# A gated delta-rule recurrence and a softplus feed-forward on one core: 64-row products for second halves, output transposes on TensorE, one queue for keys, and a new instruction order

## The chip, the cores and the metric

The kernel runs on one NeuronCore of a Trainium2 chip. The metric is the device time of one launch in microseconds (us). Engines are named as in the profile: PE is TensorE (its weight loads are listed apart as PEld), DVE is VectorE, ACT is ScalarE, POOL is GpSimd, SP is SyncE, which here only issues transfers. A letter q behind a name (SPq, POOLq) is the engine's queue of instructions that issue transfers or wait.

## The reference

Four batches of eight heads carry a 48 x 48 state through 768 steps; the gated readouts of all heads form 3072 rows of 384, which go through a feed-forward layer with softplus.

```python
k_n = k / (np.linalg.norm(k, axis=-1, keepdims=True) + 1e-06)
state = zeros((B, H, D, D))                       # B, H, S, D = 4, 8, 768, 48
for t in range(S):
    y[:, :, t] = g[:, :, t] * einsum('bhd,bhde->bhe', q[:, :, t], state)
    v_old = einsum('bhde,bhd->bhe', state, k_n[:, :, t])
    state = state + beta[t] * einsum('bhd,bhe->bhde', k_n[:, :, t], v[:, :, t] - v_old)
x = y.transpose(0, 2, 1, 3).reshape(B * S, H * D)  # 3072 x 384
h = x @ w_in                                       # w_in 384 x 2048
out = (maximum(h, 0) + log1p(exp(-abs(h)))) @ w_out   # w_out 2048 x 384
```

All inputs and the output are float32.

## The kernel before

Time is cut into 12 chunks of 64 steps. Within a chunk, the dependence of each step on earlier steps of the same chunk is a triangular system of 64 unknowns; its matrix comes from the gram products of the keys (tile kkm), and it is solved by an inverse that is built for two chunks at a time: of the two 32-step halves of each chunk directly (tile td), and of the coupling of the second half to the first by a product (tile z). Then a chain runs through the chunks: readout of the state by the keys (w), inverse times w (u), product with z, new u, new state (s), and the gated output (yg). Finally the gated output is transposed (xt), and the dense layer runs on it: `g1` products into h, softplus on ACT into ga, `g2` products into o, copy (osb), store.

Every piece of work is an item. Items carry the cost that was reckoned with when the order was made; emission follows a fixed list of words, a letter for the engine and the item's number. The cost has no effect on the instructions.

```python
def follow(self, table):
    for word in table.split():
        it = self.items[int(word[1:])]
        en = self.ENGINES[word[0]]        # P: PE, D: DVE, A: ACT, G: POOL, S: SP
        it.eng = en
        for b in it.bufs:                 # buffers are taken from rings in this order
            if b.ap is None:
                b.ap = b.ring.free.pop(0)
        it.fn(en) if it.alt else it.fn()
        # ... cut: buffers given back to their rings, counts of items
```

Each engine executes its own items strictly in the order of the list. Loads bring one chunk of q, k, v or g in two transfers of 192 KB each; weights follow on the queue of POOL, each behind a named load.

```python
BY_ACT = (("k", 0), ("k", 2))
FIRST = (("k", 1), ("k", 0), ("k", 2), ("k", 3), ("q", 0), ("v", 0), ("g", 0), ("v", 1), ("q", 1), ("g", 1))
W_IN = (("q", 0), ("q", 0), ("v", 0), ("v", 0))
W_OUT = (("v", 1), ("v", 1), ("q", 1), ("q", 1))
Y_DMA = 4
# ...
r_kn = ring("kn", 4, [P, 2, H, 64], F16, init=pad0)
r_k = ring("kf", 3, [P, 2, H, D], F32)
r_q = ring("qf", 2, [P, 2, H, D], F32)
r_v = ring("vf", 3, [P, 2, H, D], F32)
r_g = ring("gf", 3, [P, 2, H, D], F32)
r_z = ring("z", 3, [P, U, HC], F16)
r_xt = ring("xt", 2, [P, 4, 3, P], F16)
p_d = ring("d", 5, [P, 512], F32, psum)
p_h = ring("h", 2, [P, 512], F32, psum)
p_o = ring("o", 1, [P, 512], F32, psum)
# ... in load():
(nc.scalar if (name, c) in BY_ACT else nc.sync).dma_start(
    out=b.ap[64 * b2 : 64 * b2 + 64].rearrange("t p h d -> t (p h) d"),
    in_=x[2 * b2 : 2 * b2 + 2, :, t0 : t0 + C].rearrange("p h t d -> t (p h) d"),
)
```

The inverse of a pair of chunks runs in steps of two operations, on DVE for the first pair, on POOL for the others. The pair of chunks 8 and 9 takes the wide form of 31 steps:

```python
def step(j):                               # wide form, POOL
    n, w = 31 - j, j + 1
    t = tmp.ap[:, : n * w].rearrange("p (i c) -> p i c", c=w)
    nc.gpsimd.tensor_tensor(t, nn.ap[:, j + 1 :, j : j + 1].broadcast_to([P, n, w]),
                            tt.ap[:, j : j + 1, :w].broadcast_to([P, n, w]), ALU.mult)
    nc.gpsimd.tensor_tensor(tt.ap[:, j + 1 :, :w], tt.ap[:, j + 1 :, :w], t, ALU.add)

for j in range(31):
    prev = add("POOL", "step", 0.52 + 3.2e-3 * (31 - j) * (j + 1), lambda j=j: step(j), deps=[prev], ...)
```

The z-products (`zmm`). The identity puts td of the second half into the second-half rows of z; the kernel before does not read those rows:

```python
for r in range(2):
    f = QUAD[2 * r + 1]                    # rows 32..63 and 96..127
    nc.tensor.matmul(o[f], ident[f, f], td.ap[f, 16 * cl : 16 * cl + 16])   # 512 columns
for u in range(16):
    for r in range(2):
        nc.tensor.matmul(o[QUAD[2 * r], u],
                         kk_low(cs[0], kk, QUAD[2 * r + 1], 16 * cl + u),
                         td.ap[QUAD[2 * r + 1], 16 * cl + u, :])
```

The chain of one chunk. QUAD are the four groups of 32 partitions, HALF the two of 64; m is one of two calls each:

```python
def umm(m):                                # 32 products
    for pi in range(H):
        u = 16 * cl + 2 * pi + m
        for qd in range(4):
            nc.tensor.matmul(hd(up[m].ap)[QUAD[qd], pi], td.ap[QUAD[qd], u, :],
                             w1[m].ap[QUAD[qd], pi], start=(pi == 0), stop=False, ...)
# u1 = copy(up) on ACT or DVE
def zu(m):                                 # 16 products, added to up
    for pi in range(H):
        for r in range(2):
            nc.tensor.matmul(hd(up[m].ap)[QUAD[2 * r + 1], pi],
                             z.ap[QUAD[2 * r], 16 * cl + 2 * pi + m, :],
                             u1[m].ap[QUAD[2 * r], pi], start=False, stop=(pi == H - 1), ...)
# u2 = copy(up); smm: new state from u2; ymm: output; y: yg = output * g
```

The transpose of the gated output, and the dense layer:

```python
if c < Y_DMA or last:                      # chunks 0 to 3 and 11
    for p in range(2):
        def ytr(ytp=ytp, p=p):             # three 128x128 transposes on PE
            for j in range(3):
                nc.tensor.transpose(o[:, cs_], y[:, cs_], ident)
        # then xt: one copy of 128x384 on DVE or ACT
else:                                      # chunks 4 to 10
    nc.sync.dma_start(out=xt.ap[:, 2 * cl : 2 * cl + 2].rearrange("f p j t -> f (p j) t"),
                      in_=yg.ap.rearrange("t p h d -> t (p h d)"), transpose=True)
# g1: 3 products of 128x512 (pairs of chunks) or 6 of 128x256 (single chunks), 96 groups in all
# soft: Softplus on ACT, 128x512
# g2: 4 products of 128x384, 96 groups in all; o: copy on DVE or ACT; store: two transfers
```

Chunks 0, 1, 10 and 11 go through the dense layer singly, the others in pairs.

## Time and profile before

| | before |
|---|---|
| time, median of 3 | 277.19 us (276.89 to 277.89) |
| span of the profiled execution | 275.1 us, 13296 instructions |
| PE busy | 226.1 us (82%), 6030 products |
| DVE, ACT, POOL busy | 165.7 (60%), 134.8 (49%), 141.1 us (51%) |
| dense products: `g1` (h), `g2` (o) | 77.2 and 71.3 us busy, 384 each |
| softplus (ga) | 56.7 us busy, 96 operations |
| moved by DMA | 29.07 MB, 106 GB/s on average |

Busy time is from the first start to the last end of overlapping instructions of an engine; PE's products are pipelined, so that a group of them takes less than its count times the mean of one. Lines such as L236 and L238 are those of a helper that copies on ACT or on another engine, so they are told apart by their tiles (out<-in). "Idle before" is time in which the engine stood still just ahead of a group, with what ended it.

### The profile page before, as it was taken

Reading aid. Unit: us, or ns where it says so; the run is one execution under the profiler, and the core shown is the slowest. Engines: PE = TensorE matmul, PEld = TensorE weight load, DVE = VectorE, ACT = ScalarE, POOL = GpSimd, SP = SyncE. Lnnn points to the kernel's source line nnn. Section 1 sums busy time; section 2 is a strip of 40 time slices with the busy share of each in tenths; the row PEclk is TensorE's granted clock in tenths of the full one; section 3 lists DMA queues with packets and bytes.
Section 4 is the critical chain, followed back from the end, with each engine's and each line's share of the span. In section 5 each row is a group of like instructions: output and inputs, shape, how many; then the busy total and the mean of one; then the engine's idle time right before and its main releaser. Section 6 shows DMA issues by size and latency. Waiting matters only on the chain.

```text
span 275.1 us, 13296 instructions
## 1 busy us (share of the span) xinstructions
PE 226.1 (82%) x6030; PEld 150.5 (55%) x6030; DVE 165.7 (60%) x318; ACT 134.8 (49%) x230; POOL 141.1 (51%) x247
## 2 busy tenths in 40 slices
PE   0540357969898879999999999997599999999986
PEld 0430246757666555555665666553356655668754
DVE  6498589588996626896779956691757123412000
ACT  2241635433764357967447567154536356235620
POOL 8660023888917885287844788888887000000000
PEclk9999999995999979999999999999599999999999
DMA  8999999999998948455993146653312303400312
GB/s 109 144 174 193 173 164 156 181 175 150 142 160 140 135 75 169 84 104 97 151 150 61 33 90 122 116 115 59 64 27 62 76 17 63 84 14 20 71 46 61
DMA packets 113304, 29.07 MB, mean 106 GB/s; under 512 B 106464, under 2 KB 113248, under 8 KB 113248
## 3 DMA queue, kind: packets, MB, share of 16 engines
q1 hardware_dynamic: 105120, 24.19, 53.6%
q0 software_dynamic: 3968, 3.25, 7.6%
q10 hardware_dynamic: 4160, 0.79, 2.4%
q8 instruction: 47, 0.77, 1.2%
q14 instruction: 9, 0.07, 0.1%
HBM read 25.26 MB, written 4.72 MB: 109 GB/s over the span
## 4 chain that ended last, share of the span: by engine, by line
PE 39%; POOL 23%; DVE 11%; DMA 8%; issue 7%; SPq 6%; ACT 3%; DVEq 0%; POOLq 0%; ACTq 0%
PE o L1224 13%; PE h L1194 13%; SPq L268 6%; POOL t L685 6%; POOL tmp L679 6%; DMA qf<-in_q_dram 6%; POOL tt L753 4%; POOL tmp L746 4%; DVE kkm L599 3%; DMA gf<-in_g_dram 2%; PE d L1006 2%; PE d L1043 1%; DVE ln L713 1%; PE d L951 1%; PE d L882 1%
## 5 line engine op out<-in xcount | busy, mean ns | idle before, releaser
L1194 PE MATMUL h<-xt,w_in 128*128 128x512 f16 (+1 forms) x384 | 77.2, 338 | 0.9 <-ACT xt L236 0.6
L1208 ACT ACTIVATE ga<-h 128x512 f16<-128x512 f32 x96 | 56.7, 598 | 40.6 <-PE h L1194 39.3
L1224 PE MATMUL o<-w_out,ga 128*128 128x384 f16 x384 | 71.3, 329 | 1.3 <-DVE osb L238 0.7
L1224 PEld LDWEIGHTS <-ga 128*128 128x128 f16 x384 | 35.8, 98 | 24.4 <-issue 1.9
L1194 PEld LDWEIGHTS <-w_in 128*128 128x128 f16 x384 | 35.6, 101 | 22.6 <-issue 3.3
L433 PE MATMUL d<-ident,kn 128*128 128x128 f16 x96 | 9.4, 258 | 19.6 <-ACT kn L236 10.0
L753 POOL TENSOR_TENSOR tt<-tt,tmp 128x30 f32<-128x30 f32 (+7 forms) x60 | 23.1, 385 | 4.7
L746 POOL TENSOR_TENSOR tmp<-nn,tt 128x30 f32<-128x30 f32 (+7 forms) x60 | 22.0, 367 | 4.5
L236 ACT ACTIVATE u<-d 128x384 f16<-128x384 f32 x28 | 13.3, 492 | 21.8 <-PE d L1043 10.9
L236 ACT ACTIVATE kqx<-d 128x512 f16<-128x512 f16 x27 | 15.0, 593 | 16.2 <-PE d L433 13.4
L599 DVE TENSOR_TENSOR kkm<-d,both 128x512 f16<-128x512 f32 x32 | 20.5, 676 | 2.1 <-PE d L589 2.1
L236 ACT ACTIVATE osb<-o 128x384 f32<-128x384 f32 x19 | 9.3, 489 | 25.2 <-PE o L1224 23.1
L995 DVE TENSOR_TENSOR w<-vf,d 128x384 f16<-128x384 f32 x22 | 11.4, 548 | 15.3 <-ACT ga L1208 11.0
L330 POOL TENSOR_TENSOR ksq<-kf 128x768 f32<-128x768 f32 x6 | 9.1, 1522 | 22.3 <-DMA gf<-in_g_dram 18.5
L433 PEld LDWEIGHTS <-kn 128*128 128x128 f16 x96 | 7.5, 116 | 22.6 <-ACT kn L236 11.8
L238 DVE CAST u<-d 128x384 f16<-128x384 f32 x20 | 10.8, 553 | 14.1 <-PE d L1006 9.4
L363 POOL TENSOR_TENSOR nv<-nv,half_c 128x32 f32<-128x32 f32 x3 | 16.3, 5445 | 5.4 <-DVE nv L340 5.4
L685 POOL TENSOR_TENSOR t<-t,tmp 128x31 f32<-128x31 f32 (+15 forms) x31 | 17.1, 551 | 2.4
L679 POOL TENSOR_TENSOR tmp<-n,t 128x31 f32<-128x31 f32 (+15 forms) x31 | 16.7, 539 | 2.4
L1128 DVE TENSOR_TENSOR yg<-d,gf 128x384 f16<-128x384 f32 x24 | 12.4, 550 | 6.3 <-PE d L1106 6.3
L238 DVE COPY osb<-o 128x384 f32<-128x384 f32 x5 | 2.8, 553 | 20.8 <-PE o L1224 20.8
L1093 DVE TENSOR_TENSOR s<-d,s 128x384 f16<-128x384 f32 x20 | 10.4, 551 | 7.8 <-PE d L1076 7.8
(112 smaller groups left out, 376.8 us busy)
## 6 DMA issues: line engine op xcount, KB each, us to landing
qf<-in_q_dram SPq DMA_DIRECT2D x24, 192.0 KB, 5.6
vf<-in_v_dram SPq DMA_DIRECT2D x24, 192.0 KB, 5.6
gf<-in_g_dram SPq DMA_DIRECT2D x24, 192.0 KB, 4.7
out_dram<-osb SPq DMA_DIRECT2D x48, 96.0 KB, 3.1
kf<-in_k_dram SPq DMA_DIRECT2D x20, 192.0 KB, 5.6
w_in<-in_moe_w_in_dram POOLq DMA_DIRECT2D x4, 384.0 KB, 10.8
w_out<-in_moe_w_out_dram POOLq DMA_DIRECT2D x4, 384.0 KB, 6.5
kf<-in_k_dram ACTq DMA_DIRECT2D x4, 192.0 KB, 6.0
```

Source lines behind the costliest of these rows:

```text
L236: nc.scalar.activation(o, x, AF.Copy, scale=float(sign))
L268: (nc.scalar if (name, c) in BY_ACT else nc.sync).dma_start(out=b.ap[64 * b2 : 64 * b2 + 64].rearrange("t p h d -> t (p h) d"), in_=x[2 * ...
L363: nc.gpsimd.tensor_tensor(x, x, half_c[:, sl], ALU.pow)
L433: nc.tensor.transpose(f16ps(tp.ap)[:, P * i : P * i + P], n.ap.rearrange("t p h d -> t (p h d)")[:, P * i : P * i + P], ident,)
L599: nc.vector.tensor_tensor(kkm.ap[:, u0 : u0 + 7 : 2], gb[m].ap.rearrange("p (n t) -> p n t", t=2 * C), both[:, None, :].broadcast_to([P, N ...
L679: nc.gpsimd.tensor_tensor(t, nn.ap[:, j + 1 :, j : j + 1].broadcast_to([P, n, w]), tt.ap[:, j : j + 1, :w].broadcast_to([P, n, w]), ALU.mult,)
L685: nc.gpsimd.tensor_tensor(tt.ap[:, j + 1 :, :w], tt.ap[:, j + 1 :, :w], t, ALU.add)
L746: eng.tensor_tensor(t, nn.ap[:, :, j + 1 :, j : j + 1].broadcast_to([P, 2, n, w]), tt.ap[:, :, j : j + 1, 16 : 16 + w].broadcast_to([P, 2, ...
L753: eng.tensor_tensor(rows, rows, t, ALU.add)
L1194: nc.tensor.matmul(hp.ap[:, n * b : n * b + n], w_in[:, j, f * P : (f + 1) * P], xt.ap[:, t0 // P : (t0 + n) // P, j], start=(j == 0), sto ...
L1208: lambda hp=hp, o=gb: nc.scalar.activation(o.ap, hp.ap, AF.Softplus),
L1224: nc.tensor.matmul(op.ap[:, :DM], b.ap[:, col + c0 : col + c0 + 128], w_out[:, f, :], start=(f == 0), stop=(f == NF - 1),)
```

## The change

Four parts:

1. The inverse of the second half of a chunk is no longer applied by a separate 32-row product. `umm` forms first halves only and copies the second half of w through with an identity; `zu` then multiplies 64 rows of z, whose second-half rows hold td, with 64 rows of u1, and writes the second half of u afresh instead of adding to it.
2. The gated outputs of chunks 4 to 10 are transposed on PE and copied by DVE or ACT, as those of the other chunks were; the DMA transposes go.
3. The keys of chunks 0 and 2 are loaded by the queue of SP like all others, not by that of ACT.
4. Two cost constants of the inverse's steps are raised, and the list of words is a new one: on each engine the items stand in another order, some items go to another engine (copies, casts, squares, scalings of v), and the rings' buffers are dealt out accordingly.

```diff
-    BY_ACT = (("k", 0), ("k", 2))
+    BY_ACT = ()
...
-    Y_DMA = 4
+    Y_DMA = 12
...
-                "POOL", "step", 0.52 + 3.2e-3 * (31 - j) * (j + 1), lambda j=j: step(j),
+                "POOL", "step", 0.67 + 3.2e-3 * (31 - j) * (j + 1), lambda j=j: step(j),
...
-                en, "step", (0.42 if on_dve else 2 * fix) + 4 * per * (15 - j) * (j + 1), lambda j=j: step(j),
+                en, "step", (0.42 if on_dve else 0.6) + 4 * per * (15 - j) * (j + 1), lambda j=j: step(j),
...
         def umm(m):
+            for r in range(2):
+                f = QUAD[2 * r + 1]
+                nc.tensor.matmul(hd(up[m].ap)[f], ident[f, f], w1[m].ap[f])
             for pi in range(H):
                 u = 16 * cl + 2 * pi + m
-                for qd in range(4):
-                    nc.tensor.matmul(
-                        hd(up[m].ap)[QUAD[qd], pi],
-                        td.ap[QUAD[qd], u, :],
-                        w1[m].ap[QUAD[qd], pi],
-                        start=(pi == 0),
-                        stop=False,
-                        skip_group_check=True,
-                    )
+                for r in range(2):
+                    f = QUAD[2 * r]
+                    nc.tensor.matmul(hd(up[m].ap)[f, pi], td.ap[f, u, :], w1[m].ap[f, pi])
...
                 for r in range(2):
                     nc.tensor.matmul(
                         hd(up[m].ap)[QUAD[2 * r + 1], pi],
-                        z.ap[QUAD[2 * r], 16 * cl + 2 * pi + m, :],
-                        u1[m].ap[QUAD[2 * r], pi],
-                        start=False,
-                        stop=(pi == H - 1),
-                        skip_group_check=True,
+                        z.ap[HALF[r], 16 * cl + 2 * pi + m, :],
+                        u1[m].ap[HALF[r], pi],
                     )
...
 _TABLE = """
-S1 S0 A3 D111 P112 A2 D104 P105 G134 D135 A114 D107 A113 G132 S8 D133 A106 P115 P108 S6 D110 S9
-...
+S1 S0 A111 P112 A114 D113 P115 S3 S2 D104 A132 P105 A116 D133 S5 S4 D197 P198 A117 D107 A106 P108
+...
 """
```

The list has 1137 words before and 1158 after. Of what it changes, these places bear on the prediction (a name with the number of its chunk, or of the first of its pair; cast, red, w, s, y, kev and so on are the copies and operations named above):

```text
SP, before:   k1 k1 q0 k3 q0 k3 q1 v0 v0 g1 q1 g1 k4 q2 g0 g0 q4 q4 q2 k4 v1 v1 ...   (ACT: k0 k0, later k2 k2)
SP, after:    k1 k1 k0 k0 k2 k2 q0 q0 q1 q1 v0 v0 k3 q4 k3 g0 q4 k4 k4 v1 g0 q2 ...
DVE, before:  ... 15 steps of the first inverse, tn, t, cast q1, xs, w0, kkm, w0, red, z0, ln2 ...
DVE, after:   kev1 cast-k0 red cast-k2 kev0 ... 15 steps, tn, t, xs, w0 w0, td, kkm, mask, mask, red, z0 ...
POOL, before: square, square, 2 weight loads, square, 3 weight loads, square, cast k4, ...
POOL, after:  square, 3 weight loads, cast q4, weight load, cast k4, square, clear, weight load, ...
PE, groups of the dense layer + other groups before:    gram 9     z-products of 8    end
   before:                                              56 + 119   108 + 152          192 + 197
   after:                                               56 + 121   108 + 161          192 + 211
```

## The prediction

> **What bounds the kernel now.** I read the slices of the span first, to see which engine is busy when; then the windows of 10 us, for the idle time of TensorE; then the chain of work that ended last and the waits, for what ends that idle time; then the timeline at those places.

> ```profile
> PE   0540357969898879999999999997599999999986
> POOL 8660023888917885287844788888887000000000
> PEclk9999999995999979999999999999599999999999
> DMA  8999999999998948455993146653312303400312
> ```

> A slice is 6.88 us. TensorE is nearly empty for six slices (41 us), part filled to slice 15 (104 us), then full to the end but for a notch at slices 28 and 29. GpSimd is busy until just after that notch and then never again. The DMA engines are full for 90 us. So there are three stages: a head in which loads and the first inverse starve TensorE, a middle in which TensorE and GpSimd run side by side, and a tail that is TensorE alone.

> ```profile
> 20.00:30.00 10.00, 1.65 (x57) 1.25 (x58) 8.94 (x33) 1.93 (x3) 0.00 (x0) 1.00 1.23 192
> 30.00:40.00 10.00, 3.66 (x251) 3.12 (x241) 7.03 (x12) 5.88 (x10) 1.46 (x1) 1.00 0.99 165
> 90.00:100.00 10.00, 7.09 (x251) 5.23 (x252) 3.77 (x8) 3.71 (x8) 8.32 (x22) 0.91 0.88 124
> 160.00:170.00 10.00, 10.00 (x273) 6.22 (x270) 6.68 (x16) 6.85 (x14) 8.82 (x16) 1.00 0.45 86
> 190.00:200.00 10.00, 5.41 (x142) 2.90 (x139) 5.09 (x7) 4.40 (x6) 8.60 (x22) 0.69 0.31 56
> ```

> Columns: window, its length, busy time of PE, weight loads, DVE, ACT, POOL, then clock, DMA share, GB/s. Idle TensorE over all windows is 49 us: 28.2 before 40 us, 10.6 from 40 to 100, 10.2 after. Of the last, 4.6 lie in 190 to 200, where the clock also falls to 0.69.

> ```profile
> 33.92 0.56 DVE L238 CAST qn<-qf 128x768 f16<-128x768 f32 x1 [2.71 <-DMA qf<-in_q_dram]
> 34.40 0.42 DVE L238 CAST xs<-d 128x256 f16<-128x256 f32 x1
> ```

> That is the head's worst wait. The first inverse ended on DVE at 31.2 us, but the list has DVE cast q of chunk 1 next, whose transfer lands at 33.9; xs, which the first chunk needs, stands behind it. The first dense product is issued only at 49.9 us.

> ```profile
> 192.39 1.25 DVE t L696
> 193.67 1.97 ACT td L701
> 196.50 0.69 PE d L1006 x64
> 197.75 2.67 PE h L1194 x6
> ...
> 216.44 2.06 PE o L1224 x12
> 218.50 1.29 PE h L1194 x6
> ```

> In the chain of work (start, length, engine, tile, line), the inverse of chunks 8 and 9 runs on GpSimd from 153.8 to 192.4 us; its transpose and cast end at 195.6, where TensorE has waited 4.6 us. The next six dense products take 2.67 us at the lower clock, against 1.29 for six alike at 218.5.

> [...] in 20 to 30 us, with several issuers' transfers outstanding, traffic is 192 GB/s, and the queue of SyncE takes 6.58 us to issue one load of q, where its fastest issues take 0.6. So moving two key loads to one queue changes which bytes come first, not how many per second. [...] weight loads here show 0.2 to 0.4 us of "issue" idle at most changes of product kind, so a count of products is not the whole cost of a short group.

> **The change part by part.**

> *64-row products.* The two calls of `umm` together go from 64 products to 36. The chain shows the 64 in 0.61 us (9.5 ns each), so 16 small ones are 0.15 us. Each call adds an identity product 384 columns wide in each row half. The like exists in `zmm`: two 512-wide and 32 small take 0.59 us, less 32 x 9.5 ns = 0.28 for the wide ones, so 0.21 at 384 columns. New call 0.36, old 0.305: about +0.05 us, times 24 calls = +1.3 us, an estimate. `zu` keeps 16 products (0.25 us a call); twice the rows should cost nothing. The built program has 588 fewer TensorE instructions (24 x 28 less, 14 x 6 more), 5%, which I count as zero.

> *Gated outputs on PE.* Seven chunks lose one DMA transpose (4.1 us to land, 1.2 us of queue issue) and gain six 128x128 transposes and two evictions. Eight such transposes take 0.55 us in the chain of work (69 ns each), so 42 are 2.9 us of TensorE time. The 14 evictions of 0.35 (DVE) or 0.49 us (ACT) are 5 to 7 us, on engines busy 60% and 49%, beside other work. The DMA transposes were not waited for by TensorE anywhere that matters, so what goes is worth little by itself. Together: +4.2 us of TensorE work.

> *The head of the new list.* Order of arrival becomes k1, k0, k2, q0, q1, v0; q1 is complete as the 10th transfer instead of the 15th, and its cast is on ACT behind the first u. Nothing stands between the end of the first inverse and xs on DVE: 2.7 us gained. Three weight loads instead of five go out before the loads of the first 30 us: two times 0.39 MB at some 170 GB/s is 4.6 us of transfer time put back. DVE no longer evicts the first chunks' products before its inverse (two of 0.69 us), so that starts about 2 us sooner. Against this, casts of k0 and k2 stand in line with k2's arrival, and the fourth weight load waits behind the cast of q4, which I put at 30 us from bytes moved so far; its landing 10 us later is at 40. So the first dense product could come at 42 to 46 us. Not all of this lasts: the second inverse on GpSimd starts after the key load of chunk 5, about 51.8 against 53.3 us; but q7, for which GpSimd sat 7.3 us to 83.8, is complete as load 42 instead of 48 (6 x 0.2 MB at 155 GB/s, 7.5 us). I count -5 us, give or take 4.

> *The middle and the notch.* The list was made with a cost for each item, and two constants change. For the wide inverse the old sum is 31 x 0.52 + 17.5 = 33.6 us, the new one 38.2; the trace has 153.8 to 192.4, 38.6. The list of before thus seems to have expected td 5 us sooner than it came, about the 4.6 us hole. The new constants fit. The built order still has 52 dense groups between the grams of chunk 9 and the z-products of chunk 8, but 40 other groups instead of 33, among them four of the new transposes. So about 2 us of the added work falls into the hole, and most of the rest of the hole should close by the earlier head. I count -3.5 us of waiting and -1.5 of clock.

> *The tail.* 84 dense groups stand after that point in both lists, at 0.65 us each 54.6 of 79.4 us. Six of the new groups of transposes lie here, 1.2 us, in full on the path.

> Sum: -5 - 3.5 - 1.5 + 4.2 = -5.8, and some 0.9 us for loads and stores no longer held up behind the DMA transposes (SyncE waited 11.4 us to issue those, seldom to harm): -6.7. 277.2 - 6.7 = 270.5 us.

> **The rivals.** First: the head gains but TensorE does not. GpSimd's chain of inverses, casts and roots is the bound of the middle, and it takes three more scalings of v (1.47 us each) before the wide inverse; the hole moves to another place and only the added TensorE work remains. For it speaks that GpSimd is at 80 to 90% from 50 to 208 us; against it that 7.3, 5.4 and 4.5 us of its idle time there were waits for data. It would make 275 to 280. Second: a new list brings new mispredicted waits. Its DVE cast of k2 ahead of k0's eviction, GpSimd's cast of q4 ahead of a weight load, and loads of q6 moved from 37th to 57th place are bets on the landing of transfers, as the cast of q1 was, and this one cost 2.7 us. One or two such would make 273 to 278. Third, in the other direction: the head gives the whole 8 us between 50 and 42, the hole closes, and the waits of 40 to 100 us (10.6 idle) shrink with it: 262 to 265.

> **Range and chances.** Head 4, middle 3 and unforeseen waits 3 us, taken as independent, are about 5.8 us; 8 in 10 is 1.28 times that, 7. I take 263 to 277.5. Two per cent below is 271.6, one us above my number, so faster by 2% is little better than even: 0.54. Slower than 282.7 takes two rivals at once: 0.08. The rest, 0.38, is within.

> **What would show each step.** Right: the first dense product near 44 us and no DVE wait for q1; TensorE idle before the first z-products of chunk 8 under 2 us with its clock near 1 there; `umm` calls near 0.36 us; 72 transposes at the line that had 30, and from that point to the end still about 80 us. Wrong: a first dense product after 48 us (head), a hole of over 3 us anywhere after 100 us (middle), or `umm` groups far from the sum, or softplus late behind evictions on ACT (a new bound that I gave nothing).

## The result, and the profile after

The changed kernel takes 268.56 us (median of 4 executions, 266.97 to 270.14) against 277.04 us: a ratio of 0.969, with a 95% interval of 0.962 to 0.976. The prediction was 270.5 us, in a range of 263 to 277.5. Its sum was 1.9 us off; what the sum is made of was further off than that, and one line of it that was set to zero turned out to govern several of the experiments. In all that follows, ratios leave disturbed executions out, while the profiled execution of four runs (32-row products, 32-row with shift, shift by 64, two queues) was such a one, 2 to 5 us longer than the ratio would have it.

The slices of the span, the rows that were shown of before. A slice is now 6.64 us.

```profile
PE   0440477879878899999999998999999999999993
POOL 8310218588958897698858888888683200000000
PEclk9999999977998999999999999999999999999999
DMA  7999999999999579952985153160082410040212
```

The notch at slices 28 and 29 is gone from PE and from the clock; what is left of low clock is at slices 9, 10 and 13. GpSimd still falls silent near slice 31, but PE no longer has a hole there. The same five windows of 10 us (window, length, busy time of PE, weight loads, DVE, ACT and POOL, clock, DMA share, GB/s):

```profile
20.00:30.00 10.00, 0.66 (x64) 0.57 (x64) 8.87 (x29) 1.17 (x2) 0.00 (x0) 1.00 1.05 169
30.00:40.00 10.00, 7.49 (x268) 5.97 (x269) 6.66 (x13) 6.13 (x10) 2.37 (x4) 1.00 1.27 160
90.00:100.00 10.00, 9.36 (x283) 6.73 (x279) 8.98 (x18) 6.30 (x12) 9.06 (x16) 1.00 0.65 104
160.00:170.00 10.00, 9.08 (x224) 5.99 (x219) 5.91 (x12) 3.41 (x7) 8.98 (x14) 1.00 0.20 36
190.00:200.00 10.00, 10.00 (x343) 6.43 (x328) 6.04 (x13) 4.62 (x9) 8.35 (x21) 1.00 0.59 103
```

PE gains 3.8 us of work between 30 and 40 us, 2.3 between 90 and 100, and 4.6 between 190 and 200, where its clock is 1.00. Idle time of PE is 40.9 us in all, against 49.0: 25.6 before 40 us (before: 28.2), 9.2 from 40 to 100 (10.6), 6.1 after (10.2).

The head, in DVE's timeline: DVE stands idle for 0.28 us until PE's first products with the inverse are in, and xs follows at 29.70 us instead of 34.40. No wait for q of chunk 1 is left there. Over the first 40 us the DMA engines move 158 GB/s, with all keys on SP's queue, against 160 in before.

```profile
29.70 0.42 DVE L238 CAST xs<-d 128x256 f16<-128x256 f32 x1 [0.28 <-PE d L820]
30.05 1.02 DVE L964 TENSOR_TENSOR w<-vf,nv 128x384 f16<-128x384 f32 x2
```

The notch, in PE's timeline: the z-products of chunk 8 (L879, L882) of before, behind 4.59 us of idle time, and then of after, where dense groups run up to them and no idle time is noted in brackets.

```profile
195.68 0.61 PE L879 MATMUL d<-td,ident 32*32 32x512 f16 x2 [4.59 <-ACT td L701]
```

```profile
186.21 1.46 PE L1188 MATMUL h<-xt,w_in 128*128 128x512 f16 x6
187.50 0.81 PE L1218 MATMUL o<-w_out,ga 128*128 128x384 f16 x4
188.26 0.39 PE L879 MATMUL d<-td,ident 32*32 32x512 f16 x2
188.27 0.58 PE L882 MATMUL d<-td,kkm 32*32 32x32 f16 x32
```

And one line of the DMA queues that the prediction did not look at. Columns: packets, MB, share of 16 engines. Of before, then of after:

```profile
q8 instruction: 47, 0.77, 1.2%
```

```profile
q8 instruction: 45, 0.74, 1.3%
```

A product of PE is two instructions, a weight load and the product: 2 x 6030 / 47 = 257 instructions a packet before, 2 x 5736 / 45 = 255 after, 16 KB each. So about one packet of this queue comes for every 256 instructions of PE. I call 256 of them a block and its packet a fetch; that the packets bring PE's program is my reading of the count and of the stops. In PE's timeline of before:

```profile
95.17 0.30 PE L1006 MATMUL d<-w,td 32*32 32x48 f16 x19
97.84 0.25 PE L1006 MATMUL d<-w,td 32*32 32x48 f16 x13 [2.38 <-issue]
```

PE stops in the middle of a group of 32 like products, with no data to wait for. The trace's records place the stop at instruction 4031, which is 191 of its 256, and a packet of q8 landed 1.66 us earlier. The seven other gaps of before at 191, of 0.35 to 1.25 us from one start to the next, ended 1.44 to 1.64 us behind a landing. In every trace of this study, all stops of PE over 0.6 us after 30 us that the profile puts down to issue fall at numbers 189 to 191 of 256. I call this place the border of a block, and the stops border stalls.

### The profile page after: what moved, and what is told of

It reads as the page before. It is cut to its first block, busy times and chain, and to the rows that moved or that the text cites. A ratio compares the mean times of both kernels' runs of the same rounds, so it can differ in the third digit from the quotient of the medians.

```text
span 265.7 us, 12724 instructions
## 1 busy us (share of the span) xinstructions
PE 224.8 (85%) x5736; PEld 150.7 (57%) x5736; DVE 162.6 (61%) x317; ACT 141.1 (53%) x242; POOL 144.0 (54%) x250
## 4 chain that ended last, share of the span: by engine, by line
PE 72%; DVE 15%; DMA 5%; issue 2%; ACT 2%; SPq 2%; POOL 0%; DVEq 0%; ACTq 0%; POOLq 0%
PE o L1218 24%; PE h L1188 22%; PE d L433 4%; PE d L1040 3%; PE d L951 3%; PE d L1100 3%; DMA w_out<-in_moe_w_out_dram 2%; DMA kf<-in_k_dram 2%; DVE ln L713 2%; SPq L268 2%; PE d L1141 2%; PE d L1010 2%; PE d L1070 2%; PE d L882 2%; DVE tt L753 1%
## 5 line engine op out<-in xcount | busy, mean ns | idle before, releaser
L1188 PE MATMUL h<-xt,w_in 128*128 128x512 f16 (+1 forms) x384 | 75.6, 332 | 2.5 <-ACT xt L236 1.2
L1218 PE MATMUL o<-w_out,ga 128*128 128x384 f16 x384 | 72.5, 330 | 1.8 <-DMA w_out<-in_moe_w_out_dram 1.3
L753 POOL TENSOR_TENSOR tt<-tt,tmp 128x30 f32<-128x30 f32 (+7 forms) x60 | 22.5, 375 | 4.7
L236 ACT ACTIVATE kqx<-d 128x512 f16<-128x512 f16 x33 | 18.9, 600 | 10.6 <-DVE kqx L238 6.2
L238 DVE CAST u<-d 128x384 f16<-128x384 f32 x20 | 11.0, 555 | 20.2 <-PE d L1040 12.1
L973 POOL TENSOR_TENSOR vf<-vf,nv 128x768 f32<-128x768 f32 x9 | 14.1, 1575 | 12.7 <-DMA vf<-in_v_dram 12.7
L820 PE MATMUL d<-tn,kkm 16*32 16x16 f16 x640 | 6.0, 171 | 10.9 <-ACT tn L800 10.7
L238 DVE COPY osb<-o 128x384 f32<-128x384 f32 x6 | 3.3, 558 | 17.0 <-PE o L1218 17.0
```

The source lines that it names most:

```text
L236: nc.scalar.activation(o, x, AF.Copy, scale=float(sign))
L238: ENG[en].tensor_copy(o, x)
L753: eng.tensor_tensor(rows, rows, t, ALU.add)
L1188: nc.tensor.matmul(hp.ap[:, n * b : n * b + n], w_in[:, j, f * P : (f + 1) * P], xt.ap[:, t0 // P : (t0 + n) // P, j], start=(j == 0), sto ...
L1218: nc.tensor.matmul(op.ap[:, :DM], b.ap[:, col + c0 : col + c0 + 128], w_out[:, f, :], start=(f == 0), stop=(f == NF - 1),)
```

## The experiments

The table holds all twelve runs. The ratio is against the kernel before on the same chip. Idle is span less busy time of PE. Stalls are the gaps over 0.3 us between starts of two successive PE instructions at numbers 188 to 191 of 256, after 30 us. Clock is the time lost to a clock below 1, summed over windows of 2 us from 30 to 264 us. These three are of the one profiled execution. Profiled executions stand up to 3 us from their kernel's median and those four further; so spans, stalls and clock losses are compared only roughly.

| run | ratio (95%) | span | PE busy | PE idle | stalls | clock |
|---|---|---|---|---|---|---|
| before | 1 | 275.1 | 226.1 | 49.0 | 8.0 | 8.5 |
| after | 0.969 (0.962 to 0.976) | 265.7 | 224.8 | 40.9 | 4.3 | 5.1 |
| before, short inverse | 0.980 (0.976 to 0.984) | 268.4 | 224.2 | 44.2 | 8.2 | 6.8 |
| after, short inverse | 0.977 (0.973 to 0.981) | 270.5 | 225.9 | 44.6 | 7.0 | 3.4 |
| before, hole filled | 1.005 (1.003 to 1.007) | 274.0 | 227.5 | 46.5 | 8.1 | 10.2 |
| before, q1 later | 1.002 (0.998 to 1.005) | 273.3 | 226.6 | 46.7 | 7.2 | 10.2 |
| before, 64-row | 1.006 (1.003 to 1.008) | 275.8 | 224.7 | 51.1 | 11.0 | 6.8 |
| after, 32-row | 1.015 (1.009 to 1.021) | 282.8 | 231.1 | 51.7 | 18.8 | 10.2 |
| before, outputs by PE | 1.008 (1.005 to 1.012) | 277.2 | 229.1 | 48.1 | 7.8 | 6.8 |
| after, outputs by DMA | 1.009 (1.006 to 1.013) | 277.7 | 225.5 | 52.2 | 8.8 | 11.9 |
| after, two queues for keys | 1.005 (1.002 to 1.007) | 278.3 | 223.2 | 55.1 | 8.0 | 0.0 |
| after, shift by 64 products | 0.992 (0.989 to 0.996) | 275.5 | 230.8 | 44.7 | 13.1 | 8.5 |
| after, shift by 128 products | 0.974 (0.969 to 0.979) | 266.7 | 228.5 | 38.2 | 7.5 | 3.4 |
| after, 32-row, shift by 76 | 1.003 (1.000 to 1.006) | 280.6 | 233.0 | 47.6 | 16.8 | 8.6 |

### Is GpSimd's inverse the bound, before and after?

Both kernels with the last 7 of the 31 wide steps left out, so that the inverse of chunks 8 and 9 is left unfinished.

```diff
         def step(j):
+            if j > 23:
+                return
             n, w = 31 - j, j + 1
```

> The kernel before with the last 7 of the 31 steps of the wide inverse left out (the output of chunks 8 to 11 is then not the reference's). GpSimd ends it about 6.5 us sooner. If the hole at 195.7 us costs what the prediction put it at (4.6 us of waiting, 1.5 of clock): -5 to -6 us on 277.0. If TensorE meets another wait soon after: -1 to -3.

> The changed kernel with the same 7 steps left out. If its middle is bound by TensorE, as its trace says (no idle time before the z-products of chunk 8): 0 to -0.5 us on 268.6. If GpSimd still sets the pace: -2 us or more.

Before gains 2.0%, 5.6 us; after gains nothing (0.977 against 0.969 with all steps; the intervals overlap). The window of 190 to 210 us of before with the short inverse shows why: PE 19.51 of 20 us busy, clock 1.00, where before it had 15.41 and 0.83.

```profile
190.00:210.00 20.00, 19.51 (x679) 12.62 (x678) 11.20 (x20) 11.00 (x18) 12.85 (x27) 1.00 0.30 63
```

So the hole at 195.7 us was paid for at the end in full, and in the changed kernel this inverse is not the bound. The first rival of the prediction falls.

### Filling the hole by hand

Before, with 4 groups of `g1`, their softplus, and one group of `g2` moved from behind the z-products of chunk 8 to in front of them. Words of the list alone:

```diff
-... td(8) zmm(8) ... g1 soft ... g1 soft ... g1 soft ... g1 soft ... g2 ...
+... g1 soft g1 soft g1 soft g1 soft g2 td(8) zmm(8) ...
```

> The kernel before with its whole work, and the order changed in one place: four g1 groups and one g2 group of the dense layer, with their softplus ahead of the cast of td, stand before the z-products of chunk 8 instead of after (5 x 0.65 = 3.3 us of work for the 4.6 us hole). The hole falls to some 1.3 us and the clock stays up: -3.3 us of waiting, -1.5 of clock, 272 to 273. If the chain of chunks 8 and 9, not the dense work, sets the end: 0.

It missed: 1.005, a little slower. PE's timeline shows the hole at 1.86 us instead of 4.6, as meant, and then a new stop 5 us later:

```profile
193.50 0.39 PE L879 MATMUL d<-td,ident 32*32 32x512 f16 x2 [1.86 <-ACT td L701]
...
196.22 0.50 PE L1043 MATMUL d<-u,z 32*32 32x48 f16 x15
198.67 0.19 PE L1043 MATMUL d<-u,z 32*32 32x48 f16 x1 [1.95 <-issue]
```

That is a border stall of 2 us: with 16 dense products fewer behind it, the order from there on is cut elsewhere, among small products. The clock is at 0.74 from 190 to 210 us, lower than with the whole hole (0.83). So the hole gives 2.7 us, the stall takes 2.0 and the clock another 1.7, a loss of 1.0 against the 1.3 us measured. The hole was worth what was expected only where the order behind it did not change.

### The head

Before, with DVE's cast of q of chunk 1 behind the first w, so that xs does not wait for it.

```diff
-... tn t cast(q1) xs w0 kkm w0 red ...
+... tn t xs w0 kkm w0 cast(q1) red ...
```

> The kernel before with one item moved: DVE casts q of chunk 1 after the two w of chunk 0, instead of before xs. xs and w come up to 2.7 us sooner. If the head's gain is carried to the end: -2.5 us on 277.0. If what follows on GpSimd and the loads decide (second inverse at 53.3 us, the hole at 195.7): -0.5 to 0 us, with the first dense product 1 to 2.7 us sooner.

The time is the same, 1.002 with an interval across 1. The wait of 2.7 us was real and is gone: xs stands at 31.82 us instead of 34.40, and the first state product of chunk 0 is 2.5 us sooner. That of chunk 1 is not (63.95 us against 63.81). Some 1.8 us of the lead are left when chunk 1 begins its products, and two border stalls, longer than in before (1.08 and 0.27 us at the same places), take the rest. PE's timeline:

```profile
57.73 0.41 PE L951 MATMUL d<-s,kqx 48*64 48x48 f16 x29 [1.61 <-issue]
...
63.93 0.25 PE L1106 MATMUL d<-u,kkm 64*64 64x48 f16 x2 [1.72 <-issue]
```

After, with the keys of chunks 0 and 2 on ACT's queue. The words stand where they stood; only the letter changes.

```diff
-S1 S0 A111 P112 A114 D113 P115 S3 S2 D104 ...
+S1 S0 A111 P112 A114 D113 P115 A3 A2 D104 ...
```

> The changed kernel with the loads of the keys of chunks 0 and 2 issued by the Activation engine's queue, as in the kernel before; all else as in the changed kernel, and PE's instructions are the same, block for block. Theory: the first keys come 0.5 us earlier or later at most, and what the head gains is waited off again at the inverse of chunk 1, as the run with later queries showed: 268 to 270 us, within 1 us of the changed kernel. Rival (the one queue for the keys is what brings the head forward): 2 to 3 us longer than the changed kernel, 270.5 to 272 us.

It missed by far: 1.005, some 10 us longer than the changed kernel. ACT's timeline has the reason:

```profile
6.05 0.84 ACT L236 ACTIVATE kn<-kf 128x768 f16<-128x768 f32 x1 [3.75 <-DMA kf<-in_k_dram]
8.02 0.60 ACT L236 ACTIVATE kqx<-d 128x512 f16<-128x512 f16 x1 [1.12 <-PE d L433]
8.03 1.44 ACTq L268 DMA_DIRECT2D kf<-in_k_dram  x2
```

ACT's queue issues the keys of chunk 0 at 8.03 us, behind what the list has ACT do first: a cast at 6.05 us, which waited 3.75 us for the keys of chunk 1, and a copy at 8.02. In before, the list had the loads of chunk 0 at the head of ACT's queue, and they were issued at 1.01 us:

```profile
1.01 1.55 ACTq L268 DMA_DIRECT2D kf<-in_k_dram  x2
```

So the run shows no effect of one queue or two as such; it delays the transposes of the keys of chunk 0 by 7 us and of chunk 2 by 10. The first products of the inverse come at 39.65 us instead of 28.96, and nearly all of those 10.7 us reach the end. A head late by 10.7 us costs some 10 us here.

### The outputs, by PE and by DMA

Before with all outputs transposed on PE, and after with those of chunks 4 to 10 by DMA again:

```diff
-    Y_DMA = 4                              # before
+    Y_DMA = 12
-... ydt(c) ...                             # for c = 4 to 10
+... g1 g2 ytr(c) ytr(c) xt(c) xt(c) ...    # between dense groups
```

```diff
-    Y_DMA = 12                             # after
+    Y_DMA = 4
-... ytr(c) ... ytr(c) ... xt(c) ... xt(c)  # for c = 4 to 10
+... ydt(c) ...
```

> The kernel before with all gated outputs transposed on PE, its own order, the transposes put one to four dense groups behind the gated output, 12 of the evictions of chunks 5 to 10 and one of chunk 4 on DVE, one on ACT. The prediction's term: +2.9 us of TensorE work, of which what stands ahead of the z-products of chunk 8 (eight groups, 1.6 us) falls into the 4.6 us hole: +1.3 us. Rival, the DMA transposes were held up by or held up other transfers: 0 or a gain of 1 to 3 us. Rival, the evictions delay the chain on DVE: +3 us or more.

> The changed kernel with the gated outputs of chunks 4 to 10 transposed by DMA as before, each issued at the place in the list where its first PE transpose stood. TensorE does 2.9 us less. If that work is in full on the path (no hole is left in the changed kernel): -2.9 us on 268.6. If the landing of the transposes (4.1 us) is waited for, since the order was made without it: +1 to +4 us.

Before loses 0.8%, 2.3 us (1.4 to 3.2), and PE is busy 3.0 us longer: the predicted 2.9 us of added work. The hole before the z-products of chunk 8 takes 1.6 us of it (3.01 us are left of 4.59), as expected, yet the loss is above the +1.3 us that were expected. After loses far more by the opposite edit, 4% or some 11 us, where +1 to +4 were expected. Its waits of PE (engine, line, what for; total, times, longest, in us):

```profile
PE o L1218 <- ACT osb L236: 3.6, 4, 2.9
PE h L1188 <- DMA xt<-yg: 3.6, 2, 1.9
...
PE d L1040 <- issue: 1.6, 2, 1.4
```

The dense layer now waits 3.6 us for DMA transposes, and 2.9 us for a buffer of osb behind a store; border stalls double and 11.9 us of clock are lost. The new list leaves no room for a transpose that takes some 4 us to land (2.8 to 5.0 here); how much of the 11 us is due to that and how much to moved borders is not shown.

### The products of 64 and of 32 rows

Each of the two kernels with the other's `umm` and `zu`, all else as it was. For before, shortened (after has the reverse):

```diff
 def umm(m):
+    for r in range(2): matmul(up[QUAD[2r+1]], ident, w1[QUAD[2r+1]])
     for pi in range(H):
-        for qd in range(4): matmul(up[QUAD[qd], pi], td[QUAD[qd], u], w1[QUAD[qd], pi])
+        for r in range(2): matmul(up[QUAD[2r], pi], td[QUAD[2r], u], w1[QUAD[2r], pi])
 def zu(m):
-    ... z.ap[QUAD[2 * r], ...], u1[m].ap[QUAD[2 * r], pi], start=False ...
+    ... z.ap[HALF[r], ...], u1[m].ap[HALF[r], pi] ...
```

> The kernel before, with the 64-row products alone (its own order list). The prediction's sum (identity products and small ones one after the other, +0.05 us a call): umm pairs of 0.72 us against 0.62, time +1.3 us on 277.0. The trace of the changed kernel, where a pair of umm calls takes 0.52 us (196.34 to 196.86): the wide identity products run beside the small ones, -0.1 us a pair, 12 pairs, time -1 us. A third view, that short groups are hidden anyway: 0.

> The changed kernel with the 32-row products of before, all else kept. By the prediction's sum -1.3 us on 268.6; by the changed kernel's trace +1 us, as the mirror of the run before it; hidden: 0.

The first came out at 1.006, +1.6 us. That is near the +1.3 us of the prediction's sum, but by luck: PE's busy time does not rise, it falls by 1.4 us, and stalls are 3.0 us longer (11.0 against 8.0). The second missed by more than ten times its stated size: 1.015 against 0.969, about 13 us. PE's timeline shows where some of them go:

```profile
82.17 0.65 PE L847 MATMUL d<-td,xs 32*16 32x16 f16 x64
84.74 0.45 PE L552 MATMUL d<-kqx 48*64 48x64 f16 x32 [1.93 <-issue]
85.12 0.38 PE L1006 MATMUL d<-w,td 32*32 32x48 f16 x32
85.43 0.83 PE L1194 MATMUL h<-xt,w_in 128*128 128x256 f16 x6
86.19 0.39 PE L879 MATMUL d<-td,ident 32*32 32x512 f16 x2
86.19 0.59 PE L882 MATMUL d<-td,kkm 32*32 32x32 f16 x32
86.61 0.38 PE L1006 MATMUL d<-w,td 32*32 32x48 f16 x24
89.02 0.27 PE L1006 MATMUL d<-w,td 32*32 32x48 f16 x8 [2.02 <-issue]
```

Two stops, 4.28 us apart, and between them 32 + 32 + 6 + 2 + 32 + 24 = 128 products, 256 instructions with their weight loads. The records of the q8 queue give the parts: PE crosses the border at 84.74; the next fetch begins 1.49 us later, takes 1.32, and PE goes on 1.47 us after it landed. So this block took 4.28 us from stall to stall; one of before that lies between two stalls took 4.00 (87.64 to 91.65 us). It is no fixed least: before passes one in 3.72 us without a stall (from 116.55 us), and the run with half a block more, below, one in 1.96 (from 221.12 us), where a fetch had begun 1.6 us before PE crossed the border. What sets the start of a fetch, no run shows. Small products at 9.5 ns each, the prediction's figure, would go through a block in 1.2 us; `g2` products, four of which take 0.65 us in both kernels, need 21. So, as an estimate from these figures and the 4.28 us, a block that holds some 20 dense products beside its small ones (20 x 0.163 + 108 x 0.0095 = 4.3 us) leaves no stall. How the borders cut the list can outweigh how many instructions there are: the run of before with 64-row products has 672 instructions less, but a border now falls among the small products of chunk 1, with a stop of 3.74 us at one place:

```profile
58.49 0.34 PE L1040 MATMUL d<-u,z 64*32 64x48 f16 x13
62.58 0.23 PE L1040 MATMUL d<-u,z 64*32 64x48 f16 x3 [3.74 <-issue]
```

### Moving the borders alone

To test this apart from any work, small products were put into PE's long wait for the first inverse: 64 (128 instructions, half a block) and 128 (a whole block). The third run does it to the 32-row version.

```diff
-    def fill(prio):
+    def fill(prio, n=40):
         hp = Buf(p_h)                      # PSUM tile that nothing reads
-            for _ in range(40):
+            for _ in range(n):
                 nc.tensor.matmul(hp.ap[:32, :16], ident[:32, :32], ident[:32, :16])
+    fill(0, 64)                            # or 128, or 76
 _TABLE = """
-... gramk(2) xmm(0) ...
+... gramk(2) fill xmm(0) ...
```

> As the run with 64 more products, but with 128: 256 instructions more, one whole block, so that every later block border falls where it fell in the changed kernel. Theory (instruction fetch): the stalls are those of the changed kernel again, 0 to +1.5 us against it, 268 to 270 us, though this run has twice the added work of the other. Rival 1 (each added instruction costs, wherever it stands): twice what 64 products cost. Rival 2 (only work and waits for data count): 0 to +0.5 us, as for 64 products. It is the pair that tells the three apart: long and short for the theory, long and longer for rival 1, short and short for rival 2.

> The changed kernel with 32-row products (the run that took 282.2 us) with 76 more small products in the same idle stretch at 18.2 us, so that its block borders move by 152. Theory (instruction fetch): the same working over that run's trace gives 19 us of stalls as it was and 13 us for this shift, the least that a single shift can give; 4 to 6 us shorter than without it, 276 to 278.5 us, though it has more work. Rival (the 32-row products themselves, or waits for data in a list made for other durations, cost the 13.6 us): no change, 281 to 283 us.

Half a block costs 2.4% (0.992 against 0.969), some 6.5 us, in an idle stretch where the products themselves cost nothing; a whole block, with twice the added products, costs nothing that can be told (0.974, interval 0.969 to 0.979). Neither rival predicts such a pair. The size expected for the first, 8 to 15 us, was too large: the working asked 4.1 us of every block, an estimate that lies between the 4.00 and 4.28 us above, and several blocks of these runs took less. The 32-row version gains 1.2% (3.4 us) by having more to do; 4 to 6 were expected. With the whole block, a border falls into the padding itself, and PE's timeline, from the seventh of the 128 products on, shows the stall without any operand to blame:

```profile
17.86 3.37 PE L909 MATMUL h<-ident 32*32 32x16 f16 x121
23.94 0.19 PE L909 MATMUL h<-ident 32*32 32x16 f16 x1 [2.72 <-issue]
28.62 0.55 PE L820 MATMUL d<-tn,kkm 16*32 16x16 f16 x51 [4.49 <-ACT tn L800]
```

With half a block there is, among ten others, this stall, and low clock comes with it. First PE's timeline, then windows (length, busy time of PE, clock, DMA share, GB/s):

```profile
141.20 1.05 PE L820 MATMUL d<-tn,kkm 16*32 16x16 f16 x110
144.00 0.30 PE L820 MATMUL d<-tn,kkm 16*32 16x16 f16 x18 [1.75 <-issue]
```

```profile
140.00:144.00 4.00, 2.25 (x147) 0.92 1.00 159
144.00:148.00 4.00, 4.00 (x29) 0.50 0.27 58
148.00:152.00 4.00, 4.00 (x20) 0.72 0.00 0
```

With a pause of 1.75 us the clock is at half from 143.4 to 150.2 us: 6.8 us, 3.4 lost. If that loss is put down to it, the stall comes to some 5 us. The length of a pause did not decide it in these runs: one of 2.65 us in before with 64-row products (194.12 to 196.77 us) is followed by no loss of clock.

No run of the study is faster than the changed kernel.

## Why the prediction was right, and where it was not

**Head, predicted -5 us.** The mechanism was there: xs 4.7 us earlier, first dense product at 46.45 us against 49.89 (42 to 46 was predicted). The size was not: PE's idle time is 2.7 us less by 40 us and 3.3 by 50. The first state product of chunk 0 is 6.6 us earlier and that of chunk 1 only 1.7, but this is in good part the new order, which has PE do 40 dense products before the latter, not 18. Chunk 2 is at -3.8, chunk 4 at -6.0. That a lead in the head can be lost to border stalls, the run with the later cast of q1 shows.

**What brought the rest.** Between chunks 1 and 4 before had its border stalls (1.25, 1.17 and 2.56 us the largest); the largest of after there is 0.71. Over the span stalls fall from 8.0 to 4.3 us. Clock losses fall from 8.5 to 5.1, but all of that is the hole's: between chunks 1 and 4 both kernels have half clock for 6.8 us and again for 3.4. The step that failed is "588 fewer TensorE instructions, 5%, which I count as zero". The number of them is indeed worth little; where the borders of 256 fall is worth 6.5 us in the one pair of runs that moved nothing else, more than any other term of the sum. The new list seems to have them where they hurt least: laying borders every 256 instructions over the times of the changed kernel's trace, and asking 4.1 us of each block, the stalls sum to 1.2 us as it is, and to some 4 to 19 us when the borders are moved by 16 to 240. This is an estimate, and too high where it was put to the test (15 us more for half a block, 6.5 measured). The same holds for before (2.5, and 4 to 22), and not for mixtures of the two (9 for before with 64-row products, 19 for after with 32-row ones, each over its own trace). That both lists were chosen by times on a chip would explain it; no run shows it. It is also why undoing a part of the change told little of that part.

**Notch, predicted -5 us with its clock.** Right in place and cause. The 4.6 us of idle time are gone (3.5 were counted), and the clock is 1.00 from 190 to 200 us: before was at half clock for 6.8 us there, 3.4 lost, where 1.5 were counted. From the z-products of chunk 6 to those of chunk 8 the lead grows from 4.3 to 7.4 us, with the added transposes already paid, and from there to the end it grows by another 2.0: the clock's 3.4, less some 1.2 for the transposes behind. That the list's cost constants now fit is argued from the sums; that the hole was GpSimd's and was paid in full is shown by the short inverse.

**`umm`, predicted +1.3 us.** The sign was wrong. Where the two calls follow each other, the pair takes 0.52 us from its first product to the start of the next group, not 0.72, against 0.60 before. The identity products (L1005), 0.33 us each, run beside the small ones (L1010) instead of ahead of them. PE's timeline of before, then of after:

```profile
168.09 0.67 PE L1006 MATMUL d<-w,td 32*32 32x48 f16 x64
168.69 0.50 PE L1224 MATMUL o<-w_out,ga 128*128 128x384 f16 x2
```

```profile
196.34 0.34 PE L1005 MATMUL d<-w,ident 32*32 32x384 f16 x2
196.35 0.34 PE L1010 MATMUL d<-w,td 32*32 32x48 f16 x13
...
196.86 0.82 PE L1218 MATMUL o<-w_out,ga 128*128 128x384 f16 x4
```

A call that stands alone takes 0.31 us in both. Some seven of the 12 chunks have their calls in a pair, so the gain is about 7 x 0.08 = 0.6 us. (The prediction's pauses of weight loads of 0.2 to 0.4 us are in the trace of before at 65 of 187 changes of their shape, if 0.15 to 0.45 us are counted, not at most.) That twice the rows in `zu` cost nothing holds: a product takes 178 ns with 32 rows in before and 179 with 64 in after, and 32 of them 0.57 us in both.

**Outputs on PE, predicted +2.9 and -0.9 us.** The work of the first is right, 3.0 us more PE busy time; in the old list it cost 2.3 us. The second is not shown by any run.

**Tail, predicted "still about 80 us".** 77.4, against 79.4 before; the difference is the clock, less the added transposes.

**The sum.** Predicted -6.7, measured -8.5. Spans give -9.4: idle time -8.1 and busy time -1.3, of which the clock is -3.4 and work +2.1 (transposes +3.0 and `umm` -0.6, as counted above, make 2.4). In idle time the hole gives 4.6, border stalls 3.7 and the head 2.7 up to 40 us, 11.0 together, so that some 2.9 us of other waits are new. The head gave less than was put down, `umm`, stalls and clock gave what it lacked: that the sum was only 1.9 us off is in part luck.

**Rivals.** A new bound on GpSimd: refuted. New mispredicted waits: they exist, and are small (PE waits at most 1.3 us at a time for w_out and td, 1.2 for xt, 0.9 for ga). The head's full gain: not reached.

What stays open: how much of the 8.5 us is due to the order as such and how much to where its borders fall. A list with the same order and borders placed well by other means was not tried.

## What to carry to other kernels

Where PE runs hundreds of products of 10 ns, count its instructions in blocks of 256 and look for those with little work: blocks between two stalls took 4.00 and 4.28 us here, though others passed in 3.72 and 1.96 without one. A stop put down to issue in the middle of a group of like products, with a landing of the instruction queue some 1.5 us before it (1.44 to 1.66 in before), was the sign here. Before a change of a few products is judged slower or faster, run it with some idle products ahead that move the borders by half and by a whole block (0.992 and 0.974 here): if these differ, the place of the borders is part of what was measured. And a load given to another engine's queue must be moved in the order too: on ACT's queue the keys of chunk 0 were issued at 8.03 us behind ACT's first wait, and at 1.01 us where the list had them first.

## What the runs showed of the hardware that was not expected

- In after with 32-row products, of two border stalls in a row the second came 4.28 us after the first: 1.5 from the border to the start of the next fetch, 1.3 for the fetch (0.9 to 1.6 for the others of before and after), some 1.5 from its landing to the next instruction. Another block (shift by 64 products), with a fetch begun 1.6 us before PE crossed its border, was passed in 1.96 us.
- A PE pause of 1.75 us (shift by 64 products) came with 6.8 us at half clock, and so did one of 1.05 us (shift by 128 products, to 83.06 us); one of 2.65 us (before with 64-row products) did not.
- Products with an identity, 32 rows and 384 columns, overlap 32 x 32 products on other rows of PE in the changed kernel: a pair of calls with 4 of the first, 0.33 us each, and 32 of the second takes 0.52 us. One call, with 2 and 16, takes 0.31 us, as 32 of the second alone do in before.
